# The last block of zeros in ten short transfers on SyncE's queue, and the epilogue written out twice

## The chip, the cores and the metric

One Trainium2 chip, one core. The metric is the device time of one execution, in microseconds (us); lower is better. A profiled execution gives a trace of all engines and of the core's 16 DMA engines; its span begins and ends a little inside the measured time.

## The reference

The kernel computes one decode step of a small block and all its gradients: layer norm of x, attention of one query per head over the last W = 4096 rows of a key/value cache of 32768 rows, a squared-ReLU MLP as a gate, and the vector-Jacobian product of the whole.

```python
q = (xn @ wq).reshape(B, Sq, Hq, Dh)                    # B 2, Sq 1, D 512, Hq 32, Hkv 8, Dh 128
k, v = k_cache[:, :, Sk - W:], v_cache[:, :, Sk - W:]   # W 4096 of Sk 32768
s = softmax(q k^T * Dh**-0.5) v @ wo
g = silu(relu(xn @ w1 + b1)**2 @ w2 + b2)               # w1 512 x 1792, w2 1792 x 512
out = x + s * g
grads = vjp(out, (x, k_cache, v_cache, wq, wo, w1, b1, w2, b2))(grad_out)
```

The outputs are out_0 (the forward result), out_1 (gradient of x), out_2 and out_3 (gradients of the two caches), out_4 (wq), out_5 (wo), out_6 and out_7 (w1, b1), out_8 and out_9 (w2, b2). All are bf16. out_2 and out_3 have the caches' size, 2 x 8 x 32768 x 128 each; only the last 4096 rows of each head take part in the attention, so the other 28672 rows (ZR in the code) of each of the 32 (output, batch, head) blocks are zeros that have to be written.

## The kernel before

The kernel is written in a tile language: instructions of one engine run in the order in which a scheduler put them, semaphores are placed by it, and writes to one output tensor, or reuse of one tile, are kept in order by waits.

**The zeros.** A tile of zeros, zt, lies in SBUF (L80). At the start 31 of the 32 zero blocks are queued from GpSimd (POOL), each as one or several DMAs, through the helper zf (L101), which keeps their handles in sw_fill. At most eight of them are in flight, by eight semaphores, so POOL's queue is fed for most of the run. The thirty-second block, the last head of out_3, is written by one SP DMA at the very end of the program (L641): 128 partitions by 4 repeats by 7168 elements. It is told to be issued after the store of out_6 (issue_after) and depends on the last but one fill of POOL (sw_fill[-2]).

**The work.** Weights are loaded on SP's queue, then four rounds go over the heads in groups of four. A round loads a slice of V and K (SP, L217), computes scores and gradients, and stores the slices of out_3 and out_2 (ACT's queue, L422). In the last round the output row, the MLP's backward pass and small outputs follow.

**The end.** After the rounds, ACT's queue stores out_4 from the tile wq (L581). Then come, in the program's text:

- L583 to L587: 32 matmuls of one 128x512 tile each; each result goes through one of three PSUM buffers (ps_o) into the tile wo by evac, which alternates between ACT (L157) and DVE (L159); ACT's queue stores wo as out_5 (L587).
- L589 to L602: a tile dw in the buffer of V's slices; in two halves, 7 transposes and a copy (L597, L598), and 7 transposes and a strided copy (L601, L602), through one PSUM buffer (ps_m).
- L605 to L610: 14 matmuls and evac into w2T; SP stores it as out_8 (L610).
- L611 to L616: 16 matmuls and evac into dw.
- L618 to L634: the layer norm's backward pass on small 128x8 tiles (dxnT, prodT, t1), with two sums over partitions by bsum (L165, L166) and four transposes (L177); SP stores the row as out_1 (L634).
- L636: SP stores dw as out_6; L641: SP writes the last zeros.

The scheduler mixes these: the layer norm part (L618 to L634) runs before most of the 32 matmuls of out_5. On SP the order is L634 (out_1), L610 (out_8), L636 (out_6), L641 (zeros).

Of the kernel before, what the change touches and what calls it, by code (L numbers as in the profile page):

```python
# [9 lines left out]
ALU = mybir.AluOpType  # L10
AX = mybir.AxisListType
BF16 = mybir.dt.bfloat16
F32 = mybir.dt.float32
# [3 lines left out]
def kernel(  # L17
# [24 lines left out]
    nc = tc.nc  # L42
    P = 128
    B, _, D = A_x.shape
    _, HKV, SK, DH = A_k_cache.shape
    N = A_wq.shape[1]
# [3 lines left out]
    F = B_w1.shape[1]  # L50
    FK = F // P
    DK = D // P
    NJ = N // P
# [3 lines left out]
    NCB = W // PB  # L57
# [11 lines left out]
    dma_store = nc.scalar  # L69
# [5 lines left out]
    ps_m = ctx.enter_context(tc.tile_pool(name="ps_m", bufs=1, space=PSUM))  # L75
    ps_o = ctx.enter_context(tc.tile_pool(name="ps_o", bufs=3, space=PSUM))

    ZR = SK - W
    ZG = 112
    zt = const.tile([P, ZG * DH], mybir.dt.uint8, name="zt")  # L80
    nc.vector.memset(zt[:].bitcast(F32), 0.0)

    ident_bf = const.tile([P, P], BF16, name="ident_bf")
    make_identity(nc, ident_bf[:])
    ident_f = const.tile([P, P], F32, name="ident_f")
    make_identity(nc, ident_f[:])

    sw_fill = []

    def zf(o, q, r0, nent, rows, rep=1):  # L90
        b, hk = divmod(q, HKV)
        nr = nent * rows * rep
        v = o[b, hk, r0:r0 + nr, :]
        w = rows * DH
        if w > ZG * DH:
            v = v.bitcast(F32)
            w //= 2
        v = v.rearrange("(r p g) d -> p r (g d)", p=nent, g=rows)
        st = 4 if nent < 16 else 1
        zs = zt[0:nent * st:st, 0:w].unsqueeze(1).to_broadcast([nent, rep, w])  # L100
        sw_fill.append(nc.gpsimd.dma_start(out=v, in_=zs))  # L101
        return r0 + nr

    ZQ = 2 * B * HKV
    zparts = [(out_2, q) for q in range(B * HKV)] + [(out_3, q) for q in range(B * HKV)]
# [12 lines left out]
    for qi in range(ZQ - 1):  # L118
        r = 0
        whole = (P, ZR // P, 1) if qi in zlong else (P, ZG, ZR // (P * ZG))  # L120
        for n, rows, rep in zshort.get(qi, (whole,)):
            r = zf(*zparts[qi], r, n, rows, rep)
# [8 lines left out]
    goT = const.tile([P, DK, B], F32, name="goT")  # L131
    xnT_f = const.tile([P, DK, B], F32, name="xnT_f")
    xnT = const.tile([P, DK, B], BF16, name="xnT")
    rstdb = const.tile([P, B], F32, name="rstdb")
    xn_bf = const.tile([B, D], BF16, name="xn_bf")
    w1T = const.tile([P, FK, D], BF16, name="w1T")
    w2T = const.tile([P, DK, F], BF16, name="w2T")
    rT = const.tile([P, FK, B], F32, name="rT")
    h2T_bf = const.tile([P, FK, B], BF16, name="h2T_bf")
# [3 lines left out]
    ds_rows = const.tile([B, D], BF16, name="ds_rows")  # L143
# [4 lines left out]
    dxqT = const.tile([P, DK, B], F32, name="dxqT")  # L148
# [3 lines left out]
    def evac(out_ap, in_ap, eng=None):  # L152
        if eng is None:
            eng = "act" if (evac_flip[0] % 2 == 0) else "dve"
            evac_flip[0] += 1
        if eng == "act":
            nc.scalar.copy(out=out_ap, in_=in_ap)  # L157
        else:
            nc.vector.tensor_copy(out=out_ap, in_=in_ap)  # L159

    def bsum(out_ap, in_t):
        pp = ps_m.tile([P, B], F32, tag="m")
        nk = in_t.shape[1]
        for k in range(nk):
            nc.tensor.matmul(pp[:, :], lhsT=ones_f[:, :], rhs=in_t[:, k, :], start=(k == 0), stop=(k == nk - 1))  # L165
        nc.vector.tensor_scalar_mul(out=out_ap, in0=pp[:, :], scalar1=1.0 / D)  # L166

    def kb(t2):
        return t2.unsqueeze(1).to_broadcast([P, DK, B])

    def pk_rows(t):
        return t.rearrange("b (p k) -> b k p", k=DK)

    def to_rows(src_T, dt, ident, pool=ps_m, tag="m"):
        tpp = pool.tile([B, DK, P], dt, tag=tag)
        for k in range(DK):
            nc.tensor.transpose(tpp[:, k, :], src_T[:, k, :], ident)  # L177
        return tpp

    wq = wts.tile([P, DK, N], BF16, name="wq")  # L180
    wo = wts.tile([P, NJ, D], BF16, name="wo")
# [23 lines left out]
    kvp = attn.enter_context(tc.tile_pool(name="kvp", bufs=1))  # L205
# [14 lines left out]
    with tc.tile_pool(name="pw", bufs=1) as pw:  # L220
# [14 lines left out]
        tp = ps_m.tile([P, DK, B], BF16, tag="m")  # L235
# [3 lines left out]
        tp = ps_m.tile([P, DK, B], BF16, tag="m")  # L239
# [21 lines left out]
        tp = to_rows(xnT, BF16, ident_bf[:, :])  # L261
# [3 lines left out]
        for fk in range(FK):  # L265
            for k in range(DK):
                nc.tensor.matmul(hps[:, fk, :], lhsT=w1[:, k, fk:F:FK], rhs=xnT[:, k, :],
                                 start=(k == 0), stop=(k == DK - 1))
        hBT = pw.tile([P, FK, B], F32, name="hBT")
        nc.vector.tensor_tensor(out=hBT[:], in0=hps[:], in1=b1T[:].unsqueeze(2).to_broadcast([P, FK, B]),  # L270
                                op=ALU.add)
# [3 lines left out]
        for dk in range(DK):  # L275
            for fk in range(FK):
                nc.tensor.matmul(ups[:, dk, :], lhsT=w2[:, fk, dk:D:DK], rhs=h2T_bf[:, fk, :],
                                 start=(fk == 0), stop=(fk == FK - 1))
        uT = pw.tile([P, DK, B], F32, name="uT")
        nc.vector.tensor_tensor(out=uT[:], in0=ups[:], in1=b2T[:].unsqueeze(2).to_broadcast([P, DK, B]),  # L280
                                op=ALU.add)
# [15 lines left out]
        tp = to_rows(dsT_bf, BF16, ident_bf[:, :])  # L297
# [4 lines left out]
        for j0 in range(0, NJ, JG):  # L302
            woT = pw.tile([P, JG, DK, P], BF16, tag="woT", bufs=2)
            for half in range(2):
                tp = ps_t.tile([P, 8, P], BF16, tag="pt")
                for jj in range(8):
                    j, dk = divmod(half * 8 + jj, DK)
# [3 lines left out]
            for dk in range(DK):  # L311
                nc.tensor.matmul(dops[0:B, :, :], lhsT=dsT_bf[:, dk, :], rhs=woT[:, :, dk, :],
                                 start=(dk == 0), stop=(dk == DK - 1))
            evac(do_rows[:].rearrange("b (p j) -> b j p", j=NJ)[:, j0:j0 + JG, :], dops[0:B, :, :])
        tp = ps_m.tile([P, HQ, B], BF16, tag="m")
# [5 lines left out]
        for n0 in range(0, N, 512):  # L321
            qps = ps_o.tile([P, 512], F32, tag="o")
            for k in range(DK):
                nc.tensor.matmul(qps[0:B, :], lhsT=xnT[:, k, :], rhs=wq[:, k, n0:n0 + 512],
                                 start=(k == 0), stop=(k == DK - 1))
            nc.scalar.mul(out=q_rows[:, n0:n0 + 512], in_=qps[0:B, :], mul=SCALE)
        tp = ps_m.tile([P, HQ, B], BF16, tag="m")
# [11 lines left out]
        for g0 in range(0, len(jobs), 8):  # L339
            grp = jobs[g0:g0 + 8]  # L340
            tp = ps_t.tile([P, 8, P], BF16, tag="pt")
            for j, (src, _, _, _) in enumerate(grp):
                nc.tensor.transpose(tp[:, j, :], src, ident_bf[:, :])
            j = 0
            while j < len(grp):
                dst, idx, off = grp[j][1], grp[j][2], grp[j][3]
                n = 1
# [9 lines left out]
    epi = attn.enter_context(tc.tile_pool(name="epi", bufs=1))  # L357
# [72 lines left out]
    for r in range(NR):  # L430
# [36 lines left out]
        if r == NR - 1:  # L467
            o_rows = tring[0:B, 0:N]
            for h0 in range(0, HQ, 8):
                tp = ps_t.tile([B, 8, P], BF16, tag="pt")  # L470
# [3 lines left out]
            tp = ps_s.tile([P, NJ, B], BF16, tag="sd")  # L474
# [9 lines left out]
            tp = ps_s.tile([P, DK, B], F32, tag="sd")  # L484
# [13 lines left out]
            tp = to_rows(outT, F32, ident_f[:, :], ps_s, "sd")  # L498
# [15 lines left out]
            tp = to_rows(duT_bf, BF16, ident_bf[:, :], ps_s, "sd")  # L514
            du_rows = zz[0:B, D:2 * D]
# [3 lines left out]
            for fk in range(FK):  # L519
                for dk in range(DK):  # L520
                    nc.tensor.matmul(hps[:, fk, :], lhsT=w2T[:, dk, fk * P:(fk + 1) * P], rhs=duT_bf[:, dk, :],
                                     start=(dk == 0), stop=(dk == DK - 1))
            dhBT = epi.tile([P, FK, B], F32, name="dhBT")
            nc.vector.scalar_tensor_tensor(out=dhBT[:], in0=hps[:], scalar=2.0, in1=rT[:], op0=ALU.mult, op1=ALU.mult)
            dhBT_bf = epi.tile([P, FK, B], BF16, name="dhBT_bf")
# [8 lines left out]
            for k in range(DK):  # L534
                for fk in range(FK):
                    nc.tensor.matmul(xps[:, k, :], lhsT=w1T[:, fk, k * P:(k + 1) * P], rhs=dhBT_bf[:, fk, :],
                                     start=(fk == 0), stop=(fk == FK - 1))
            dxnT = epi.tile([P, DK, B], F32, name="dxnT")
# [13 lines left out]
        b, h0 = rounds[r]  # L552
        for hk in range(h0, h0 + NP) if b == B - 1 else ():
            xps = ps_m.tile([P, DK, B], F32, tag="m")
            for half in range(2):
                wqT = wsl.tile([P, 2, DK, P], BF16, tag="wqT")
                tp = ps_t.tile([P, 8, P], BF16, tag="pt")
                for jj in range(8):
                    i, k = divmod(half * 8 + jj, DK)
                    n0 = (hk * REP + i) * DH  # L560
                    nc.tensor.transpose(tp[:, jj, :], wq[:, k, n0:n0 + DH], ident_bf[:, :])
                evac(wqT[:].rearrange("q i k p -> q (i k p)"), tp[:].rearrange("q a p -> q (a p)"))
                for k in range(DK):
                    for i in range(2):
                        nc.tensor.matmul(xps[:, k, :], lhsT=wqT[:, i, k, :], rhs=dqT_all[:, hk * REP + half * 2 + i, :],
                                         start=(half + k + i == 0), stop=(half == 1 and k == DK - 1 and i == 1))
# [4 lines left out]
            tp = ps_m.tile([B, REP, P], BF16, tag="m")  # L571
# [4 lines left out]
            for k in range(DK):  # L576
                wps = ps_o.tile([P, REP * DH], F32, tag="o")
# [5 lines left out]
    for j in range(NJ):  # L583
        wps = ps_o.tile([P, D], F32, tag="o")
# [4 lines left out]
    dw = kvp.tile([P, NCB * DH], BF16, tag="v")  # L589
    dw1_st = dw[:, 0:DK * F].rearrange("p (k f) -> p k f", k=DK)  # L590
    h2_rows = dw[0:B, DK * F:DK * F + F].rearrange("b (j p) -> b j p", j=FK)
    dhB_rows = dw[0:B, DK * F + F:DK * F + 2 * F]
    for half in range(2):
        f0, f1 = half * (FK // 2), (half + 1) * (FK // 2)
        tp = ps_m.tile([B, FK // 2, P], BF16, tag="m")
# [3 lines left out]
        tp = ps_m.tile([B, FK // 2, P], BF16, tag="m")  # L599
# [5 lines left out]
    dw2_st = w2T[:].rearrange("p k f -> p (k f)").rearrange("p (j d) -> p j d", j=FK)  # L605
    for fk in range(FK):
        wps = ps_o.tile([P, D], F32, tag="o")
# [3 lines left out]
    for k in range(DK):  # L611
        for n0 in range(0, F, 512):
            n = min(512, F - n0)
            wps = ps_o.tile([P, 512], F32, tag="o")
# [4 lines left out]
    m1b = epi.tile([P, B], F32, name="m1b")  # L619
    bsum(m1b[:], dxnT)  # L620
    prodT = epi.tile([P, DK, B], F32, name="prodT")
    nc.vector.tensor_tensor(out=prodT[:], in0=dxnT[:], in1=xnT_f[:], op=ALU.mult)
    m2b = epi.tile([P, B], F32, name="m2b")
    bsum(m2b[:], prodT)
    t1 = epi.tile([P, DK, B], F32, name="t1")
# [5 lines left out]
    tp = to_rows(t1, F32, ident_f[:, :])  # L631
    gx = dw[0:B, DK * F + 2 * F:DK * F + 2 * F + D]
# [2 lines left out]

    last = nc.sync.dma_start(out=out_6.rearrange("(p k) f -> p k f", k=DK), in_=dw1_st)  # L636
    b, hk = divmod(zparts[ZQ - 1][1], HKV)
    v = out_3[b, hk, 0:ZR, :].rearrange("(r p g) d -> p r (g d)", p=P, g=ZG // 2)
    zs = zt[:].bitcast(BF16).unsqueeze(1).to_broadcast([P, 2 * ZR // (P * ZG), ZG * DH // 2])
    with tc.issue_after(last.ins):  # L640
        fin = nc.sync.dma_start(out=v, in_=zs)  # L641
# [30 lines left out]
```

## Time and profile before

| | us |
|---|---|
| median of 2 runs (766.26 and 766.47) | 766.37 |
| the profiled execution, its own time | 766.29 |
| its span | 764.5 |
| PE busy in the span | 399.7 (52%) |
| DVE busy | 275.8 (36%) |
| ACT busy | 214.5 (28%) |
| POOL busy | 35.1 (5%) |

What the DMA queues moved, from part 3 of the page (packets, megabytes, time of their packets as a share of 16 engines' span); q0 is POOL's queue, q1 SP's, q10 ACT's:

```profile
q0 software_dynamic: 8000, 227.55, 70.4%
q1 hardware_dynamic: 2696, 56.63, 19.3%
q10 hardware_dynamic: 1736, 41.95, 13.5%
```

An engine's busy share is an average over stages. The table of 40 slices shows each engine, and the mean of the 16 DMA engines, in tenths of the slice. A timeline row has the start, the length, the engine, the line, the operation and its operands; an entry such as "ACTq L587 DMA_DIRECT2D" is the issue of a transfer by an engine's sequencer. A row of waits names who waited, for whom, how long in total, how often, and the longest. The sizes of the transfers at the end are 4096 KB (out_4 and out_5 each), 1792 KB (out_8 and out_6 each), 2 KB (out_1) and 7168 KB (the zeros).

### The profile page before, as it was taken

The page shows a single profiled execution, that of the slowest core. Times are in us where ns is not written, and L with a number is a line of the kernel's source. Part 1 is how long each engine was busy: PE and PEld are TensorE (multiplying, and loading weights), DVE is VectorE, ACT ScalarE, POOL GpSimd, SP SyncE. Part 2 cuts the span into 40 slices and gives each one's busy share as a digit, 9 for nine tenths or more (in the row PEclk, how much of TensorE's full clock was granted, in tenths as well). Part 3 has the DMA queues.
Part 4 walks back from the last instruction along what each step waited for, and adds up shares of the span by engine and source line. Part 5 has one row for each costly group of instructions (what it writes and reads, how often), then busy time and mean ns, then how long its engine had stood idle before and what let it go on. Part 6 is the DMA issues. An engine that isn't in the chain of part 4 may idle for free.

```text
span 764.5 us, 9399 instructions
## 1 busy us (share of the span) xinstructions
PE 399.7 (52%) x4118; PEld 261.8 (34%) x4118; DVE 275.8 (36%) x483; ACT 214.5 (28%) x313; POOL 35.1 (5%) x67
## 2 busy tenths in 40 slices
PE   0166774848503766870486683017645938759100
PEld 0153363734102654430275430016543424232000
DVE  3034252355501346450254653003343515567100
ACT  0034441145500124560122553002142307316100
POOL 3000010010000000000000000000000000000000
PEclk9998898968755995785599577559876957555555
DMA  9999999999999999999999999999999999999998
GB/s 360 433 425 427 442 422 430 438 426 425 429 428 438 427 446 430 413 427 435 435 427 440 427 433 438 420 433 429 437 430 436 430 440 430 418 438 425 436 417 379
DMA packets 12473, 326.73 MB, mean 427 GB/s; under 512 B 2898, under 2 KB 2906, under 8 KB 2934
## 3 DMA queue, kind: packets, MB, share of 16 engines
q0 software_dynamic: 8000, 227.55, 70.4%
q1 hardware_dynamic: 2696, 56.63, 19.3%
q10 hardware_dynamic: 1736, 41.95, 13.5%
q8 instruction: 32, 0.52, 0.3%
q14 instruction: 9, 0.07, 0.0%
HBM read 45.62 MB, written 280.50 MB: 427 GB/s over the span
## 4 chain that ended last, share of the span: by engine, by line
PE 33%; DMA 32%; DVE 14%; ACT 7%; issue 6%; ACTq 0%; DVEq 0%; SPq 0%
DMA out_dram<-nat 13%; DMA nat<-in_A_v_cache_dram 8%; DMA nat<-in_A_k_cache_dram 8%; PE ov L418 5%; PE s_ps L391 4%; PE tp L384 4%; DMA b_bf<-in_B_b_dram 4%; DVE tring L159 3%; PE dp_ps L391 2%; ACT p_bf L452 2%; ACT nat L157 2%; DVE ds_bf L465 2%; DVE nat L159 2%; PE wps L585 2%; PE ps L407 1%
## 5 line engine op out<-in xcount | busy, mean ns | idle before, releaser
L384 PE MATMUL tp<-pperm,nat 128*128 128x128 bf16 x1024 | 81.9, 228 | 136.4 <-DMA nat<-in_A_v_cache_dram 117.3
L159 DVE COPY tring<-tp 128x1024 bf16<-128x1024 bf16 (+1 forms) x98 | 65.5, 689 | 177.9 <-PE tp L384 168.3
L384 PEld LDWEIGHTS <-nat 128*128 128x128 bf16 x1024 | 70.8, 102 | 142.9 <-DMA nat<-in_A_v_cache_dram 119.3
L157 ACT CAST nat<-ov 128x512 bf16<-128x512 f32 x160 | 87.4, 590 | 61.9 <-PE ov L418 61.2
L157 ACT COPY tring<-tp 128x1024 bf16<-128x1024 bf16 (+1 forms) x34 | 34.4, 1011 | 239.7 <-PE tp L384 223.1
L159 DVE CAST nat<-ov 128x512 bf16<-128x512 f32 x96 | 65.7, 690 | 54.1 <-PE ov L418 51.4
L391 PEld LDWEIGHTS <-zz 128*128 128x128 bf16 x512 | 49.6, 100 | 37.3 <-issue 31.3
L101 POOL DMA_DIRECT2D out_dram<-zt x58 | 33.5, 581 | 529.3 <-DMA out_dram<-zt 526.1
L418 PE MATMUL ov<-bd,ds_bf 128*128 128x512 bf16 x128 | 49.2, 459 | 5.6 <-DVE nat L159 3.7
L418 PE MATMUL ov<-bd,p_bf 128*128 128x512 bf16 x128 | 48.6, 452 | 4.3 <-DVE nat L159 1.4
L391 PE MATMUL dp_ps<-tring,zz 128*128 128x256 bf16 x256 | 39.2, 284 | 12.1 <-DVE tring L159 6.9
L391 PE MATMUL s_ps<-tring,zz 128*128 128x256 bf16 x256 | 39.0, 275 | 10.9 <-DVE tring L159 9.9
L407 PE MATMUL ps<-t,nat 128*128 128x16 bf16 x1024 | 29.0, 174 | 13.7 <-DVE bd L372 6.8
L407 PEld LDWEIGHTS <-nat 128*128 128x128 bf16 x1024 | 28.9, 104 | 16.6 <-issue 11.4
L159 DVE CAST wq<-wps 128x512 bf16<-128x512 f32 x16 | 11.0, 690 | 42.4 <-PE wps L578 42.2
L399 PE MATMUL tp<-ident_bf,p_bf 128*128 128x128 bf16 x64 | 7.5, 312 | 34.9 <-ACT p_bf L452 34.9
L452 ACT ACTIVATE p_bf<-e_sb,rl 32x512 bf16<-32x512 f32 x16 | 22.8, 1424 | 3.4 <-DVE rl L449 3.3
L157 ACT CAST wq<-wps 128x512 bf16<-128x512 f32 x16 | 9.3, 586 | 50.6 <-PE wps L578 50.6
L465 DVE SCALAR_TENSOR_TENSOR ds_bf<-dp_ps,delta,p_bf 32x512 bf16<-32x512 f32 x16 | 21.8, 1360 | 0.2
L418 PEld LDWEIGHTS <-ds_bf 128*128 128x128 bf16 x128 | 12.9, 107 | 20.5 <-issue 18.2
L418 PEld LDWEIGHTS <-p_bf 128*128 128x128 bf16 x128 | 12.7, 108 | 19.5 <-issue 16.4
L399 PEld LDWEIGHTS <-p_bf 128*128 128x128 bf16 x64 | 6.5, 145 | 36.0 <-ACT p_bf L452 36.0
(195 smaller groups left out, 437.6 us busy)
## 6 DMA issues: line engine op xcount, KB each, us to landing
out_dram<-zt POOLq DMA_DIRECT2D x23, 7168.0 KB, 101.3
out_dram<-nat ACTq DMA_DIRECT2D x8, 4096.0 KB, 41.4
out_dram<-zt POOLq DMA_DIRECT2D x7, 3584.0 KB, 63.4
nat<-in_A_v_cache_dram SPq DMA_DIRECT2D x4, 4096.0 KB, 32.6
nat<-in_A_k_cache_dram SPq DMA_DIRECT2D x4, 4096.0 KB, 27.3
out_dram<-zt SPq DMA_DIRECT2D x1, 7168.0 KB, 52.2
out_dram<-zt POOLq DMA_DIRECT2D x2, 3488.0 KB, 64.6
out_dram<-zt POOLq DMA_DIRECT2D x1, 6120.0 KB, 85.8
```

What stands on the lines that cost most here:

```text
L101: sw_fill.append(nc.gpsimd.dma_start(out=v, in_=zs))
L157: nc.scalar.copy(out=out_ap, in_=in_ap)
L159: nc.vector.tensor_copy(out=out_ap, in_=in_ap)
L384: nc.tensor.transpose(tp[:, j, :], nat[:, g * CC + half * CH + j, :], pperm[:].rearrange("p b k -> p (b k)"))
L391: nc.tensor.matmul(out_ps[:, half * CH * PB:(half + 1) * CH * PB], lhsT=zbuf[:, pr, o:o + R], rhs=tT[:, :, pr, :], start=(g == 0 and pr == ...
L399: nc.tensor.transpose(tp[:, cc, :], src[:, half * CH + cc].rearrange("r k b -> r (k b)"), ident_bf[:, :])
L407: nc.tensor.matmul(ps[:], lhsT=nat[:, g * CC + half * CH + cc, :], rhs=cols[half][:, cc, :, g, :], start=(half == 0 and g == 0 and cc == 0 ...
L418: nc.tensor.matmul(ov[:], lhsT=src[:, cc].rearrange("r k b -> r (k b)"), rhs=bd[:, gh * 4:(gh + 1) * 4, :], start=True, stop=True)
L452: nc.scalar.activation(out=p_bf[rb, :, :, pr], in_=e_sb[rb], func=ACT.Copy, scale=rl[rb, 0:1])
L465: nc.vector.scalar_tensor_tensor(out=ds_bf[rb, :, :, pr], in0=dp_c[rb], scalar=delta[rb, 0:1], in1=p_bf[rb, :, :, pr], op0=ALU.subtract, o ...
L585: nc.tensor.matmul(wps[:], lhsT=o_rows[:, j:N:NJ], rhs=ds_rows[:, :], start=True, stop=True)
```

## The change

After the store of out_6 the new text writes the last head's zeros by ten DMAs on SP: one over 128 partitions with three repeats of 56 rows, one over 128 with 53 rows, and eight over 1, 7, 12, 13, 14, 15, 8 and 9 partitions (every eighth of the tile's) with 1, 2, 3, 4, 5, 6, 14 and 1 rows each. Together they are the same 28672 rows. Each is told to be issued after the one before it.

Behind them the new text has the end of the kernel once more, from the 32 matmuls of out_5 to the store of out_6, with lines of its own (L651 to L705), and then the old zero DMA, now at L710. So out_5, out_8, out_6, out_1 and the zeros are computed or written twice, to the same places. In the second pass dxqT is added to dxnT a second time (L687), so the second out_1 is made of a dxnT that holds dxqT twice. Nothing of the old text is removed.

```diff
     last = nc.sync.dma_start(out=out_6.rearrange("(p k) f -> p k f", k=DK), in_=dw1_st)
     b, hk = divmod(zparts[ZQ - 1][1], HKV)
+    zb = zt[:].bitcast(BF16)
+    r = 0
+    for n, g, rep, st in ((P, 56, 3, 1), (P, 53, 1, 1), (1, 1, 1, 8), (7, 2, 1, 8), (12, 3, 1, 8), (13, 4, 1, 8), (14, 5, 1, 8), (15, 6, 1, 8),
+                          (8, 14, 1, 8), (9, 1, 1, 8)):
+        v = out_3[b, hk, r:r + n * g * rep, :].rearrange("(r p g) d -> p r (g d)", p=n, g=g)
+        zs = zb[0:n * st:st, 0:g * DH].unsqueeze(1).to_broadcast([n, rep, g * DH])
+        with tc.issue_after(last.ins):
+            fin = nc.sync.dma_start(out=v, in_=zs)
+        if r == 0:
+            tc.add_manual_dep(fin.ins, sw_fill[-2].ins.name,
+                              mybir.DependencyInfo(mybir.DependencyClass.Sync, mybir.DependencyReason.DATA))
+        last = fin
+        r += n * g * rep
+    assert r == ZR, (r, ZR)
+    for j in range(NJ):
+        wps = ps_o.tile([P, D], F32, tag="o")
+        nc.tensor.matmul(wps[:], lhsT=o_rows[:, j:N:NJ], rhs=ds_rows[:, :], start=True, stop=True)
+        evac(wo[:, j, :], wps[:])
+    dma_store.dma_start(out=out_5.rearrange("(p j) m -> p j m", j=NJ), in_=wo[:])
+
+    dw = kvp.tile([P, NCB * DH], BF16, tag="v")
...
+    for half in range(2):
...
+            nc.tensor.transpose(tp[:, j, :], h2T_bf[:, f0 + j, :], ident_bf[:, :])
+        nc.vector.tensor_copy(out=h2_rows[:, f0:f1, :], in_=tp[:])
...
+            nc.tensor.transpose(tp[:, j, :], dhBT_bf[:, f0 + j, :], ident_bf[:, :])
+        nc.vector.tensor_copy(out=dhB_rows.rearrange("b (p j) -> b j p", j=FK)[:, f0:f1, :], in_=tp[:])
...
+    nc.sync.dma_start(out=out_8.rearrange("(p j) d -> p j d", j=FK), in_=dw2_st)
...
+    nc.vector.tensor_tensor(out=dxnT[:], in0=dxnT[:], in1=dxqT[:], op=ALU.add)
...
+    nc.sync.dma_start(out=out_1.rearrange("b s d -> (b s) d"), in_=gx)
+
+    last = nc.sync.dma_start(out=out_6.rearrange("(p k) f -> p k f", k=DK), in_=dw1_st)
+    b, hk = divmod(zparts[ZQ - 1][1], HKV)
     v = out_3[b, hk, 0:ZR, :].rearrange("(r p g) d -> p r (g d)", p=P, g=ZG // 2)
     zs = zt[:].bitcast(BF16).unsqueeze(1).to_broadcast([P, 2 * ZR // (P * ZG), ZG * DH // 2])
     with tc.issue_after(last.ins):
         fin = nc.sync.dma_start(out=v, in_=zs)
```

In the order of the built program SP issues, after the first out_1, out_8 and out_6: the second out_1 (L703), out_8 (L679) and out_6 (L705), the ten zero DMAs (L645), and L710. ACT issues the second out_5 (L656) between its copies of the second pass. The semaphores that the new instructions wait for: the first copies into wo on ACT and DVE, the landing of the first out_5; the first copy into the second dw (L667), the landing of the first out_1 and out_6; the last six of the ten zero DMAs, the landing of an earlier DMA that used the same semaphore (for the ninth the first of the ten, for the tenth the second); L710, the landing of all ten.

More of the change, by code (lines that the diff above doesn't have):

```diff
@@ new lines @@
+    assert r == ZR, (r, ZR)
[5 more added lines that the diff above has]
+    dw = kvp.tile([P, NCB * DH], BF16, tag="v")
+    dw1_st = dw[:, 0:DK * F].rearrange("p (k f) -> p k f", k=DK)
+    h2_rows = dw[0:B, DK * F:DK * F + F].rearrange("b (j p) -> b j p", j=FK)
@@ new lines @@
+    dhB_rows = dw[0:B, DK * F + F:DK * F + 2 * F]
+    for half in range(2):
+        f0, f1 = half * (FK // 2), (half + 1) * (FK // 2)
+        tp = ps_m.tile([B, FK // 2, P], BF16, tag="m")
+        for j in range(FK // 2):
+            nc.tensor.transpose(tp[:, j, :], h2T_bf[:, f0 + j, :], ident_bf[:, :])
+        nc.vector.tensor_copy(out=h2_rows[:, f0:f1, :], in_=tp[:])
+        tp = ps_m.tile([B, FK // 2, P], BF16, tag="m")
+        for j in range(FK // 2):
+            nc.tensor.transpose(tp[:, j, :], dhBT_bf[:, f0 + j, :], ident_bf[:, :])
+        nc.vector.tensor_copy(out=dhB_rows.rearrange("b (p j) -> b j p", j=FK)[:, f0:f1, :], in_=tp[:])
@@ new lines @@
+    dw2_st = w2T[:].rearrange("p k f -> p (k f)").rearrange("p (j d) -> p j d", j=FK)
+    for fk in range(FK):
+        wps = ps_o.tile([P, D], F32, tag="o")
+        nc.tensor.matmul(wps[:], lhsT=h2_rows[:, fk, :], rhs=du_rows, start=True, stop=True)
+        evac(dw2_st[:, fk, :], wps[:])
+    nc.sync.dma_start(out=out_8.rearrange("(p j) d -> p j d", j=FK), in_=dw2_st)
+    for k in range(DK):
+        for n0 in range(0, F, 512):
+            n = min(512, F - n0)
+            wps = ps_o.tile([P, 512], F32, tag="o")
+            nc.tensor.matmul(wps[:, 0:n], lhsT=xn_bf[:, k:D:DK], rhs=dhB_rows[:, n0:n0 + n], start=True, stop=True)
+            evac(dw1_st[:, k, n0:n0 + n], wps[:, 0:n])
@@ new lines @@
+    nc.vector.tensor_tensor(out=dxnT[:], in0=dxnT[:], in1=dxqT[:], op=ALU.add)
+    m1b = epi.tile([P, B], F32, name="m1b")
+    bsum(m1b[:], dxnT)
+    prodT = epi.tile([P, DK, B], F32, name="prodT")
+    nc.vector.tensor_tensor(out=prodT[:], in0=dxnT[:], in1=xnT_f[:], op=ALU.mult)
+    m2b = epi.tile([P, B], F32, name="m2b")
+    bsum(m2b[:], prodT)
+    t1 = epi.tile([P, DK, B], F32, name="t1")
+    nc.vector.tensor_tensor(out=t1[:], in0=xnT_f[:], in1=kb(m2b[:]), op=ALU.mult)
+    nc.vector.tensor_tensor(out=t1[:], in0=dxnT[:], in1=t1[:], op=ALU.subtract)
@@ new lines @@
+    nc.vector.tensor_tensor(out=t1[:], in0=t1[:], in1=kb(m1b[:]), op=ALU.subtract)
+    nc.vector.tensor_tensor(out=t1[:], in0=t1[:], in1=kb(rstdb[:]), op=ALU.mult)
+    nc.vector.tensor_tensor(out=t1[:], in0=t1[:], in1=goT[:], op=ALU.add)
+    tp = to_rows(t1, F32, ident_f[:, :])
+    gx = dw[0:B, DK * F + 2 * F:DK * F + 2 * F + D]
+    nc.vector.tensor_copy(out=pk_rows(gx), in_=tp[:])
+    nc.sync.dma_start(out=out_1.rearrange("b s d -> (b s) d"), in_=gx)
+    last = nc.sync.dma_start(out=out_6.rearrange("(p k) f -> p k f", k=DK), in_=dw1_st)
```

## The prediction

> **What bounds the kernel now.** I read the page's table of 40 slices first, for which resource is never idle.
>
> ```profile
> DMA  9999999999999999999999999999999999999998
> GB/s 360 433 425 427 442 422 430 438 426 425 429 428 438 427 446 430 413 427 435 435 427 440 427 433 438 420 433 429 437 430 436 430 440 430 418 438 425 436 417 379
> HBM read 45.62 MB, written 280.50 MB: 427 GB/s over the span
> ```
>
> The DMA engines are 90% busy or more in every slice but the last, and the busiest compute engine (PE) only 52%. The kernel is bound by bytes; compute matters only if it delays the issue of a transfer when nothing else is queued. So next come the windows of the last 54 us, with compute beside DMA, and a window of the DMA queues there.
>
> ```profile
> core 0: us, PE busy (x) PEld busy (x) DVE busy (x) ACT busy (x) POOL busy (x), PEclk, DMA share, GB/s
> ...
> 711.00:720.00 9.00, 0.00 (x0) 0.00 (x0) 0.00 (x0) 0.00 (x0) 0.00 (x0) 0.50 1.02 436
> 720.00:730.00 10.00, 0.00 (x0) 0.00 (x0) 0.00 (x0) 0.00 (x0) 0.00 (x0) 0.50 1.03 437
> ...
> 745.00:750.00 5.00, 0.00 (x0) 0.00 (x0) 0.00 (x0) 0.00 (x0) 0.00 (x0) 0.50 1.02 436
> ```
>
> Compute is over at 711; 21.87 MB are still to move (DMA view, 711 to 764.5). From 744 to 750 only SP's queue (q1) moves bytes, 2.62 MB, so POOL's and ACT's queues are empty by then. The timeline says when the last transfers were issued, the waits of SP when they landed.
>
> ```profile
> 667.12 3.97 DVE L602 COPY dw<-tp 2x896 bf16<-2x896 bf16 x1 [0.40 <-PE tp L601]
> ...
> 696.63 0.35 ACTq L587 DMA_DIRECT2D out_dram<-wo  x1
> ...
> 704.18 0.33 SPq L610 DMA_DIRECT2D out_dram<-w2T  x1
> ...
> 710.84 0.33 SPq L636 DMA_DIRECT2D out_dram<-dw  x1
> 711.36 0.39 SPq L641 DMA_DIRECT2D out_dram<-zt  x1
> ```
>
> ```profile
> SPq L667 <- DMA out_dram<-zz: 27.1, 1, 27.1
> ...
> SPq L667 <- DMA out_dram<-zt: 17.0, 1, 17.0
> ...
> SPq L667 <- DMA out_dram<-wq: 4.3, 1, 4.3
> SPq L667 <- DMA out_dram<-dw: 3.0, 1, 3.0
> ```
>
> These are SP's closing waits, which begin at 711.8. Put end to end as 27.1, 4.3, 3.0, 17.0 they end at 738.9, 743.2, 746.2 and 763.2. The second agrees with out_5's own record (issued 696.63, landing after 46.6 us: 743.2). So out_5 lands at 743.2, out_6 at about 746.2, and the last fill, 7168 KB issued at 711.36, is what keeps DMA busy afterwards: 7.34 MB in 17.0 us, 432 GB/s. It lands at 763.6 (52.2 us after issue), 0.9 us before the span ends.
>
> **What the Trainium skill says.** "DMA: Bandwidth & Descriptors", section "Issuing engines are not separate DMA queues": DMAs started by SP, ACT and POOL run on the same 16 engines and interleave. The trace agrees: 437 GB/s with three queues (720 to 730), 436 with one (745 to 750). Same page, "Anatomy of one DMA — SWDGE (gpsimd) path": about 2.0 us fixed per DMA, most of it the wait for the last byte's receipt. The trace splits it for a hardware queue: the first load is issued at 0.74 and bytes flow from about 2.0 (1.3 us), and the last fill's final data packet is at about 762.7 against its landing at 763.6 (0.9 us); together 2.2 us, which I use. Same page, "Why a DMA increments its semaphore by 16 and not by 1": a hardware-queue DMA uses the largest number of engines up to 16 that divides its slowest dimension, so 7 rows use 7 engines; no row of this trace shows that.
>
> **The change, part by part.** The words speak of the last fill alone. The diff has more: after ten new fills (L645) it repeats the whole end of the kernel (out_5, out_8, out_6, out_1) and keeps the old fill, now L710. The order of the built program has both copies. Removed: nothing; the old fill moves to the end of SP's queue.
>
> (a) *Bytes.* Added are 4096 KB (out_5), 1792 (out_8), 1792 (out_6), 2 (out_1) and 7168 (ten fills): 14850 KB = 15.2 MB. At 432 GB/s: **+35.2 us**, with nothing to hide under, since DMA is full already.
>
> (b) *First pass.* In the built order seven transposes (L666) and two small DVE operations (L687, L691) slip in at about 683: 0.91 us by the like row L601, 0.17 each by L618. SP then issues the first out_6 at about 712 instead of 710.84. Free: three queues hold bytes past 740.
>
> (c) *A new wait, and the fill that covered it is gone.* The second pass refills wo, so its first copies on ACT and DVE wait for the first out_5 to have landed, 743.2. Behind them stand everything else on ACT and DVE and, through three PSUM buffers, PE. On SP the ten fills stand behind the second out_6 (L705), thus behind the whole second pass. After the first out_6's last bytes (746.2 less 0.9: 745.3) no queue holds anything.
>
> (d) *Second pass, from rows of the first, at the same 0.50 clock.* 32 wo copies: ACT's starts go from 686.49 to 695.42 in ten steps, 0.89 us a pair. The twelfth DVE copy ends about 743.2+11.1 = 754.3, then L667 0.6. The last four wo copies, held by transposes between the matmuls, end at 758.7. ACT issues the second out_5 after its next copy: 759.4. L671 (as L602, 3.97) to 762.7; copy, transposes, L667, transposes (0.91 twice, 0.6, overlap taken) to 765.2; L671 again to 769.2. The mean and variance chain as in the first pass, 677.7 to 685.3: 7.6 us, so 776.9. Remaining four pairs of out_8 copies at 0.89: 780.5, issue of the second out_8. Then 6.66 us (704.18 to 710.84): **second out_6 issued at 787.3**.
>
> DMA in that time: idle 745.3 to 760.7 (759.4+1.3), 15.4 us; out_5 4.19 MB, 9.7 us, to 770.4; idle to 781.8, 11.4 us; out_8 1.835 MB, 4.3 us, to 786.1; idle to 788.6, 2.5 us. **Idle 29.3 us.**
>
> (e) *The fills.* From 788.6 out_6 (1.835 MB), the 128x3x7168 fill (5.51 MB) and the 128x6784 one (1.74 MB) flow without a gap: 9.08 MB, 21.0 us, to 809.6. The short ones are 98 KB in all. Issues cost some 0.4 us each and lie under the flow. But the ninth waits for the semaphore of the first fill and the tenth for that of the second, which lands at 810.5. The tenth then takes 2.2: 812.7. SP issues L710 only when all ten have landed, since it writes the same rows: first byte 814.0, 17.0 us of bytes to 831.0, landed 831.9, span end 832.8. **Idle here 4.4 us.**
>
> Sum against the profiled execution: span 764.5 + 35.2 + 29.3 + 4.4 = 833.4, by the chain 832.8; I take 833. Around the span lie 766.29 - 764.5 = 1.8 us: **835 us**; the median of the two runs (766.37) is 0.1 above the profiled one. What no row shows: the fixed time of a DMA on a few engines, 1 to 4 us (it enters twice, since both the tenth and L710 start on idle queues): -2 to +4; the length of the second pass: as quick as DVE's copies alone, 0.69 for 0.89 on some 27 pairs, -5.4; as slow as the first from its first matmul (663.81 to 710.84, 47.0 instead of 44.1): +2.9. Engines that drain unevenly may move each start by a little, 2 us either way (a choice). All ends together: 825 to 844.
>
> **Rivals.**
> 1. *The second pass is covered and only the bytes count.* 766.3 + 35.2 = 802, and up to 8 us less if DMA's small losses (327 MB at 432 GB/s would take 756) were made up. It needs bytes queued between 746 and 788; the built order has the fills behind L705, against it. Chance 0.05; with a half-covered gap, 815 to 825, another 0.05.
> 2. *Waits pile up further*: engines that drain unevenly lengthen each of the landings in the chain (out_5, fill one, fill two, tenth, L710), or a pass that meets out_6's landing in L667 (746.2, before 754.3, so not expected to bind): 844 to 855. Chance 0.07.
> 3. *The other side: the change does no more than its words say*, one set of stores and short fills in place of the long one. Then only SP's tail grows: at least two dependent landings at 2.2 us, 766.3 + 4.4 = 771, within 2%. It decides if no second out_5, out_8, out_6 and no L710 is issued. Against it are the diff and the built order. Chance 0.02. No cover could bring the full change there: 15.2 MB would have to fit into 15.3 us.
>
> **How the numbers follow.** Forecast, 825 to 844: 0.81. Rival 1 with its half-way case 0.10, rival 2 0.07, rival 3 0.02. The predicted time is the likeliest case's, 835. The range 825 to 844 leaves out 0.19. Two per cent, about what a measurement can tell from no change, is 15.3 us: slower by more than that are all cases but rival 3: 0.98; same 0.015, faster 0.005.
>
> **What would show it.** Right: MB moved near 342; three near-empty stretches of DMA, about 745 to 761, 770 to 782 and 786 to 788; ACT and DVE waiting for out_dram<-wo until about 743; L656 issued near 759, L705 near 787, L710 near 813, and 17 us of SP's queue alone at the end. Wrong: DMA at 430 GB/s throughout (rival 1), no L710 (rival 3), L710 issued without waiting for the ten (2.2 us less and both flows joined), or a second pass much longer or shorter than 44 us.

## The result and the profile after

The changed kernel takes 834.09 us (two runs, 833.59 and 834.58) against 766.37 before: a ratio of 1.0884, 95% interval 1.0837 to 1.093. The forecast was 835, with a range of 825 to 844. The profiled execution has a span of 832.5 us. In three of the kernels below, one execution ran two to three per cent longer than the others (824.3, 793.88 and 792.73 us); these three are left out of the figures given.

First the page of the changed kernel, the DMA rows of its 40 slices and its bytes:

```profile
DMA  9999999999999999999999999999999999974398
GB/s 363 429 433 421 442 424 442 413 442 421 433 430 432 443 422 421 435 428 431 446 425 429 422 438 427 429 444 433 434 428 429 428 438 417 436 338 202 136 394 353
...
HBM read 45.62 MB, written 295.71 MB: 410 GB/s over the span
```

295.71 MB are written where it was 280.50: 15.2 MB more, the stores and zeros written twice. But the rate over the span has fallen from 427 to 410 GB/s, and nearly all of the fall lies in four of the 40 slices, the 36th to the 39th (a slice is 20.8 us long). Up to there the rows are much like those of before. So the time has two parts: more bytes, and a DMA that stands idle. The windows of the changed kernel show the holes (columns: stretch, its length, busy time of PE, PE loads, DVE, ACT and POOL, clock, DMA share, GB/s):

```profile
747.00:750.00 3.00, 3.00 (x8) 0.93 (x7) 2.42 (x4) 1.93 (x4) 0.00 (x0) 0.50 0.00 0
750.00:755.00 5.00, 5.00 (x13) 1.60 (x12) 3.94 (x7) 3.33 (x6) 0.00 (x0) 0.50 0.00 0
755.00:760.00 5.00, 5.00 (x16) 1.50 (x16) 3.46 (x6) 2.51 (x5) 0.00 (x0) 0.50 0.00 0
...
765.00:770.00 5.00, 1.44 (x8) 0.71 (x7) 4.60 (x4) 0.57 (x1) 0.00 (x0) 0.50 0.98 419
...
772.00:777.00 5.00, 3.75 (x15) 2.37 (x15) 1.55 (x8) 0.59 (x1) 0.00 (x0) 0.50 0.00 0
...
800.00:808.00 8.00, 0.00 (x0) 0.00 (x0) 0.00 (x0) 0.00 (x0) 0.00 (x0) 0.50 1.01 430
```

Read the last column beside the PE, DVE and ACT columns. From 747 to 760 compute works and not one byte moves; from 765 to 770 the second out_5 flows; from 772 to 777 nothing moves again; from 800 to 808 DMA is full and compute is over. In the kernel before such windows had bytes and no compute, because the last zeros were queued there. Why compute is so late is on ACT's timeline of the changed kernel:

```profile
743.97 1.07 ACT L157 CAST wo<-wps 128x512 bf16<-128x512 f32 x2 [29.90 <-DMA out_dram<-wo]
...
759.64 0.34 ACTq L656 DMA_DIRECT2D out_dram<-wo  x1
```

The second pass's first copy into wo waited 29.90 us for the first out_5 to land. And SP's timeline of the changed kernel shows what stands behind that pass:

```profile
777.90 0.26 SPq L703 DMA_DIRECT2D out_dram<-dw  x1
781.10 0.34 SPq L679 DMA_DIRECT2D out_dram<-w2T  x1
787.77 0.33 SPq L705 DMA_DIRECT2D out_dram<-dw  x1
788.15 23.32 SPq L645 DMA_DIRECT2D out_dram<-zt  x10
812.81 0.40 SPq L710 DMA_DIRECT2D out_dram<-zt  x1
```

SP's waits of the changed kernel (who, for whom: total us, times, longest) name the landings at the end:

```profile
SPq L736 <- DMA out_dram<-zt: 17.9, 1, 17.9
SPq L645 <- DMA out_dram<-zt: 12.6, 2, 8.9
...
SPq L710 <- DMA out_dram<-zt: 1.1, 1, 1.1
```

Two of the ten zero DMAs waited for another one, then L710 for the tenth, then the program for L710.

### The profile page after: what moved, and what is told of

It reads as the page before. It is cut to its first block, busy times and chain, and to the rows that moved or that the text cites. A ratio compares the mean times of both kernels' runs of the same rounds, so it can differ in the third digit from the quotient of the medians.

```text
span 832.5 us, 9725 instructions
## 1 busy us (share of the span) xinstructions
PE 443.4 (53%) x4219; PEld 280.0 (34%) x4228; DVE 307.0 (37%) x528; ACT 232.7 (28%) x344; POOL 35.0 (4%) x67
## 3 DMA queue, kind: packets, MB, share of 16 engines
HBM read 45.62 MB, written 295.71 MB: 410 GB/s over the span
## 4 chain that ended last, share of the span: by engine, by line
DMA 34%; PE 33%; DVE 14%; ACT 7%; issue 5%; ACTq 0%; DVEq 0%; SPq 0%
DMA out_dram<-nat 11%; DMA nat<-in_A_k_cache_dram 8%; DMA nat<-in_A_v_cache_dram 7%; DMA out_dram<-wo 5%; PE ov L418 5%; PE s_ps L391 4%; PE tp L384 4%; DMA b_bf<-in_B_b_dram 4%; DVE tring L159 3%; PE dp_ps L391 2%; ACT p_bf L452 2%; ACT nat L157 2%; DVE ds_bf L465 2%; PE wps L585 2%; PE wps L654 2%
## 5 line engine op out<-in xcount | busy, mean ns | idle before, releaser
L391 PE MATMUL dp_ps<-tring,zz 128*128 128x256 bf16 x256 | 40.9, 293 | 11.6 <-DVE tring L159 6.4
L159 DVE CAST wo<-wps 128x512 bf16<-128x512 f32 x32 | 22.3, 696 | 38.7 <-DMA out_dram<-wo 29.9
L157 ACT CAST wo<-wps 128x512 bf16<-128x512 f32 x32 | 18.7, 586 | 61.0 <-DMA out_dram<-wo 29.9
L654 PE MATMUL wps<-ds_rows,tring 2*128 2x512 bf16 x32 | 14.9, 606 | 29.5 <-ACT wo L157 29.4
```

The source lines that it names most:

```text
L391: nc.tensor.matmul(out_ps[:, half * CH * PB:(half + 1) * CH * PB], lhsT=zbuf[:, pr, o:o + R], rhs=tT[:, :, pr, :], start=(g == 0 and pr == ...
L654: nc.tensor.matmul(wps[:], lhsT=o_rows[:, j:N:NJ], rhs=ds_rows[:, :], start=True, stop=True)
```

## The experiments

Two theories were set against each other. Theory 1 is the prediction's: 35 us are bytes, and the rest is DMA standing idle, because the second pass waits for the first out_5 and the zeros are queued behind the pass, plus waits for landings at the end. Theory 2: the time is bytes plus what short DMAs over few engines cost by themselves. The kernel before ran beside the experiments at 766.4 to 766.5 us.

### The cover given back: the zeros ahead of the second pass

```diff
+    with tc.issue_after(fin.ins):
+        nc.sync.dma_start(out=out_8.rearrange("(p j) d -> p j d", j=FK), in_=dw2_st)
...
+    with tc.issue_after(fin.ins):
+        nc.sync.dma_start(out=out_1.rearrange("b s d -> (b s) d"), in_=gx)
...
+    with tc.issue_after(fin.ins):
+        last = nc.sync.dma_start(out=out_6.rearrange("(p k) f -> p k f", k=DK), in_=dw1_st)
```

> The second pass's stores of out_1, out_8 and out_6 are told to be issued on SP after the ten zero DMAs, so the zeros go out at about 714 and no byte or instruction is added or taken away. Theory 1 (DMA stood idle because the zeros were queued behind the second pass): the zeros fill the idle stretch from 745 to 763, the second out_5 follows to 772, out_8 runs 782 to 787, out_6 starts at 789 and the last zero DMA joins it: 789.1 + 21.2 = 810.3, landed 811.2, span 812.1, time 813.8 us. Theory 2 (the time is the bytes plus a cost of the short DMAs on few engines, wherever they stand): unchanged, 834.

Measured: 812.89 us (four runs, 812.34 to 813.16; ratio 1.0604, 1.0588 to 1.062). The same bytes and instructions take 21.2 us less in another order on SP's queue; on PE, DVE and ACT the order in the trace is that of the changed kernel. The windows of this kernel:

```profile
745.00:760.00 15.00, 14.97 (x38) 4.51 (x36) 11.43 (x17) 9.20 (x16) 0.00 (x0) 0.50 1.02 434
...
772.00:780.00 8.00, 6.24 (x21) 2.96 (x22) 4.40 (x11) 2.19 (x4) 0.00 (x0) 0.50 0.05 16
```

The stretch that had 0 GB/s has 434 beside busy engines; the later hole, before the second out_8, is still there, as forecast. Theory 2 falls here as the main cause.

### The wait taken away: the second pass in tiles of its own

```diff
-        evac(wo[:, j, :], wps[:])
+        evac(wo2[:, j, :], wps[:])
-    dma_store.dma_start(out=out_5.rearrange("(p j) m -> p j m", j=NJ), in_=wo[:])
+    dma_store.dma_start(out=out_5.rearrange("(p j) m -> p j m", j=NJ), in_=wo2)
...
-    dw = kvp.tile([P, NCB * DH], BF16, tag="v")
+    dw = kvp.tile([P, NCB * DH], BF16, tag="k")
...
-    dw2_st = w2T[:].rearrange("p k f -> p (k f)").rearrange("p (j d) -> p j d", j=FK)
+    dw2_st = w1T[:].rearrange("p j d -> p (j d)").rearrange("p (j d) -> p j d", j=FK)
```

Here wo2 is a view of the tile wq, whose store is done early.

> The second pass puts its results in other tiles (out_5 in the tile of wq, out_8 in that of w1T, its dw in the buffer of K), which are free by about 711 or earlier, so it does not wait for the landing of the first out_5 at 743. Theory 1: the pass starts at about 714 and issues its out_6 near 758 to 764, while DMA is still full; only bytes and the landings at the end remain, 766.4 + 35.2 + 4.4 = 806, 804 to 810. Theory 2 (bytes and short DMAs): unchanged, 834. Theory 3 (the second pass itself is slow, 44 us, at the low clock, wherever it starts): it would show as a pass of over 44 us, but also near 806.

Measured: a ratio of 1.0556 (1.0517 to 1.0595), which is 809 us, with runs from 806.55 to 811.7. Within the forecast's 804 to 810, at its upper end. Its windows tell why:

```profile
745.00:750.00 5.00, 4.88 (x11) 1.29 (x10) 4.02 (x6) 3.15 (x7) 0.00 (x0) 0.50 0.35 151
750.00:755.00 5.00, 4.07 (x9) 1.07 (x9) 2.83 (x5) 2.48 (x5) 0.00 (x0) 0.50 0.98 419
```

One hole of about 3 us is left. Without the wait the scheduler put pieces of the second pass into the first: the second out_1 is issued at 723.71, ahead of the first out_8, and the first out_6 only at 733.58. So the second out_5 is issued at 748.39, when the queues have run dry. Also here no byte was taken away, and 25 us are gone. But two things changed at once, the wait and the order of the passes, so the 25 us are not the price of the wait alone.

### Less to write: one of the two sets of zeros left out

Without L710 (its lines deleted; every output is still written once or more):

> The last zero DMA (L710), which writes the same rows a second time, is left out. Theory 1: the span ends when the tenth short DMA has landed, at about 812.7, plus 0.9: 813.6, time 815.3 us, 18.8 less (17.0 of bytes and one fixed time of about 2). Theory 2: 7.34 MB at 432 GB/s less: 817.1.

Measured: 815.4 us (815.11 to 815.81), the forecast being 815.3. Without the ten zero DMAs and with L710:

> The ten zero DMAs are left out, the second pass and the old zero DMA stay, so the zeros are written once. Theory 1: L710's place is right behind the second out_6 at 788.2, out_6 and zeros flow from 789.1 for 21.2 us, landed 811.2, span 812.1, time 813.8 us: 20.3 less, of which 17.0 are bytes and 3.3 the two landings that the ninth and tenth short DMA and L710 waited for. Theory 2: the bytes, 17.0, and on top whatever DMAs on few engines cost; if that is a large part of the 67.7 us, well under 810.

Measured: 813.35 us (812.42 to 813.63), forecast 813.8. So leaving out L710 saves 18.7 us and leaving out the ten saves 20.7: 17.0 are the bytes of a set of zeros, the rest landings that something waits for. Neither is near the 67.7 of the whole, so the short DMAs are not the main cost.

### Fewer bytes inside the hole

First the second out_5 was computed and not stored (the line of L656 deleted).

> The second out_5 is still computed into wo but not stored: 4.19 MB, 9.7 us of DMA at 432 GB/s, are left out. Theory 1 (between 744 and 788 the chain of compute that waited for the first out_5 sets the time, and DMA only fills holes in it): the time stays, 834 within 1.5. Theory 2 (every byte counts): 824.4.

Measured: 829.49 us (829.31 to 829.78), 4.6 less: neither 834 nor 824.4. SP's timeline of this kernel:

```profile
782.97 0.33 SPq L704 DMA_DIRECT2D out_dram<-dw  x1
...
785.94 20.72 SPq L645 DMA_DIRECT2D out_dram<-zt  x10
```

The second out_6 is issued at 782.97 instead of 787.77, 4.8 us earlier. Without that store the scheduler put the layer norm's sums among the copies of out_6 (DVE's first sum, at 775.83, comes after the last copy of out_8) and not ahead of the last copies of out_8, so the pass was another one. If half the row is stored, the order on PE, DVE and ACT stays that of the changed kernel:

```diff
-    dma_store.dma_start(out=out_5.rearrange("(p j) m -> p j m", j=NJ), in_=wo[:])
+    dma_store.dma_start(out=out_5.rearrange("(p j) m -> p j m", j=NJ)[:, 16:NJ, :], in_=wo[:, 16:NJ, :])
```

> Of the second out_5 only the second half of each partition's row is stored: 2.10 MB, 4.9 us of DMA at 432 GB/s, are left out, and PE, DVE and ACT keep the order of instructions of the changed kernel (without the store altogether they did not). Theory 1 (the chain of compute sets the time there): 834.1 within 0.8. Theory 2 (every byte counts): 829.2.

Measured: 833.96 us (832.65 to 835.1). 2.10 MB less, worth 4.9 us of a full DMA, change nothing: the bytes of the second out_5 flow inside a hole that the chain of compute holds open. Part of that chain are DVE's strided copies, for which PE's transposes and sums wait (waits of the changed kernel):

```profile
PE pp L165 <- DVE dw L671: 3.5, 1, 3.5
...
PE tp L666 <- DVE dw L671: 2.9, 1, 2.9
```

### Only what the words say

The ten zero DMAs instead of the old one, and no second pass:

> What the words of the change say and no more: the ten zero DMAs in place of the old one, no second pass, no L710. Theory 1: the zeros flow as before, but the tenth DMA waits for the landing of the second, so the end is one fixed time later: 766.4 + 2.2 = 768.6, 768 to 769.5. Theory 2: if the few-engine DMAs even out engines that end late, below 766; if they cost by themselves, over 771.

Measured: a ratio of 1.0026 (1.0015 to 1.0037), median 768.55 us, 2.0 more than the 766.53 before, as expected. This is the prediction's rival 3 as a kernel. Then with the eight short ones ahead of the two long ones, alone and in the changed kernel:

```diff
-    for n, g, rep, st in ((P, 56, 3, 1), (P, 53, 1, 1), (1, 1, 1, 8), ..., (9, 1, 1, 8)):
+    for n, g, rep, st in ((1, 1, 1, 8), ..., (9, 1, 1, 8), (P, 56, 3, 1), (P, 53, 1, 1)):
```

> As the words of the change say, without the second pass and L710, and with the eight short zero DMAs ahead of the two long ones. No short DMA waits for a long landing, the bytes are those of before. Theory 1: the time of before, 766.4 within 0.7. Theory 2 (few-engine DMAs cost by themselves): over 768.

> The eight short zero DMAs stand ahead of the two long ones; bytes, number of DMAs and partitions are the same. The two long ones then share semaphores with short ones that have landed early, and only L710 waits for a long landing. Theory 1 (each landing waited for on an empty queue costs about 2.2 us): one landing less, 834.1 - 2.2 = 831.9. Theory 2 (few-engine DMAs cost by themselves, wherever they stand): 834.

Both expectations missed: 769.56 us (769.0 to 770.23) where 766.4 was expected, and 835.72 (835.03 to 836.12) where 831.9 was. The windows of the first of these kernels, and two of SP's waits in it:

```profile
744.00:746.00 2.00, 0.00 (x0) 0.00 (x0) 0.00 (x0) 0.00 (x0) 0.00 (x0) 0.50 0.64 260
746.00:748.00 2.00, 0.00 (x0) 0.00 (x0) 0.00 (x0) 0.00 (x0) 0.00 (x0) 0.50 0.03 11
748.00:750.00 2.00, 0.00 (x0) 0.00 (x0) 0.00 (x0) 0.00 (x0) 0.00 (x0) 0.50 0.83 344
```

```profile
SPq L645 <- DMA out_dram<-wo: 18.7, 1, 18.7
...
SPq L645 <- DMA out_dram<-dw: 2.1, 1, 2.1
```

The expectation had left out that the short ones share semaphores with the stores before them. The sixth waits 18.7 us for out_5, the eighth 2.1 us for out_6. It is issued at 746.59, when the queues are empty, and the first long one stands behind it on SP and goes out at 747.38: a hole of about 3 us at 745.

In the changed kernel there is a hole too, from 793 to 796, but for another reason:

```profile
788.01 8.21 SPq L645 DMA_DIRECT2D out_dram<-zt  x10
...
794.00:796.00 2.00, 0.00 (x0) 0.00 (x0) 0.00 (x0) 0.00 (x0) 0.00 (x0) 0.50 0.10 27
```

Here no zero DMA waits: SP's waits have no row for L645. SP issues the ten without a pause, but issuing one takes it 0.28 to 1.39 us, and the eight short ones take 7.2 us together. The first long one goes out at 795.23, and by then the bytes of out_6 are through. So neither kernel tests a removed landing; one hole was exchanged for another.

Last, six short ones in place of eight, behind the long ones, so that with eight semaphores no zero DMA waits for another:

```diff
-        ..., (1, 1, 1, 8), (7, 2, 1, 8), (12, 3, 1, 8), (13, 4, 1, 8), (14, 5, 1, 8), (15, 6, 1, 8), (8, 14, 1, 8), (9, 1, 1, 8)
+        ..., (12, 2, 1, 8), (12, 3, 1, 8), (13, 4, 1, 8), (14, 5, 1, 8), (15, 6, 1, 8), (8, 14, 1, 8)
```

> The changed kernel with six short zero DMAs in place of eight (12, 12, 13, 14, 15 and 8 partitions, the same 384 rows), so that no zero DMA shares a semaphore with another one; L710 still waits for all. Theory 1: one landing on an empty queue less than in the changed kernel, 834.1 - 2.2 = 831.9, 831.4 to 832.6. Theory 2 (short DMAs cost by their number or few engines, no wait in it): at most a quarter of such a cost is gone, 833.5 or more.

> Only the zero DMAs are changed, no second pass and no L710, and with six short ones behind the two long ones, so that none of them waits for a zero DMA. Theory 1: nothing is left of the change that could cost, the time of before, 766.5 within 0.5. Theory 2 (short DMAs even out engines that end late): 765.5 or less. Theory 3 (they cost by themselves): 768 or more.

Measured: 833.48 us (832.79 to 833.97) where 831.9 was expected, and a ratio of 1.0014 (1.0008 to 1.0021), median 767.56, where 1.0 was. Both missed. In the kernel without a second pass about 1 us of the 2.0 is gone and about 1.2 stays; in the changed kernel 0.6 are gone by the medians, where 2.2 were expected. The DMA view of the changed kernel with six short ones, in the quarter and half microseconds 808.5 to 809, 809.25 to 809.5 and 809.5 to 810, and then three of its issues (KB, us from issue to landing, where the view has it), say what stays:

```profile
DMA packets 16, 0.22 MB, mean 434 GB/s; under 512 B 0, under 2 KB 0, under 8 KB 0
DMA packets 88, 0.04 MB, mean 163 GB/s; under 512 B 46, under 2 KB 88, under 8 KB 88
DMA packets 71, 0.06 MB, mean 114 GB/s; under 512 B 41, under 2 KB 63, under 8 KB 71
...
out_dram<-zt SPq DMA_DIRECT2D x1, 1696.0 KB, 22.1
out_dram<-zt SPq DMA_DIRECT2D x1, 22.5 KB, 16.4
...
811.18 0.39 SPq L710 DMA_DIRECT2D out_dram<-zt  x1
```

The last long packets start before 809 at 434 GB/s; the short rows come behind them, at 163 and 114 GB/s, and their 98 KB take from 809.2 to 810.0. The second long DMA, issued at 787.90, lands at 810.0 too. But the short one of 22.5 KB, issued at 794.50, lands at 810.9, and L710, which waits for all, is issued at 811.18. The landing records of this trace have the six short ones one after another, about 0.17 us apart, from 810.18 to 811.06. So 1.2 us pass between the landing of the last long zeros and L710, after the short rows' bytes have moved too: it is their landings in a row. That the 1.2 us of the kernel without a second pass are the same is not shown.

With the ten and no second pass, the tenth is the last to land, as expected (at 765.86 by the landing records of that trace), but the other short ones are down only at 765.19; so leaving the tenth out gives back only a part of the 2.0 us. About 1.2 us are what is left of theory 2. None of the versions beats the kernel before.

## Why the prediction was right

**What bounds the kernel** held: wherever long transfers were queued, DMA moved some 430 GB/s, and where none were, compute set the time. The sum holds term by term. From 745 to 788.6 the changed kernel moved 6.26 MB, 14.5 us at 432 GB/s, so 29.1 of these 43.6 us were idle (forecast 29.3). From 788.6 to the first byte of L710, at 813.7, it moved 9.18 MB, 21.2 us, so 3.9 were idle (forecast 4.4). With 35.2 for the bytes that is 68.2 us; the span grew by 68.0.

**(a) Bytes.** 15.2 MB more are written. The price of 432 GB/s fits the two sets of zeros (17.0 us each, plus landings).

**(b) First pass.** Free, as put. In the profiled execution the first out_6 is issued at 714.19, later than the 712 of the working, and out_5 still lands near 743. In the first experiment's trace the whole first pass is 19 us later (out_5 issued at 718.86, out_6 at 733.10), and the wait for out_5 still ends at 743.29: the time of landing hardly depended on the time of issue.

**(c) The wait and the lost cover.** Forecast at 743.2, the first copy starts at 743.97. The first experiment shows the lost cover (21.2 us by order alone). The second shows that without the wait most of the idle time goes (25 us), though in another order of the two passes.

**(d) The second pass.** Forecast issues: out_5 759.4, out_8 780.5, out_6 787.3; measured 759.64, 781.10 and 787.77. Each duration came from a row of the first pass at the same clock, including DVE's two strided copies of nearly 4 us, which hold PE and with it everything else. The idle time was right for the reason given: halving the transfer inside it changed nothing. Two small errors cancel here. The start was put 0.8 us early. And the first byte was put 1.3 us after an issue, but it comes after 0.8 to 0.9 us (out_5 issued at 759.64, first bytes at 760.5; out_6 at 787.77 and 788.6; L710 at 812.81 and 813.7). The row that the 1.3 was read from shows less, too: the first load was issued at 0.74, and SP's queue moves bytes from about 1.77, not 2.0.

**(e) The fills.** L710 was forecast at about 813 and issued at 812.81; the span ends at 832.5, forecast 832.8. The chain was the one forecast: the second zero DMA lands, the tenth is issued at 810.72 and L710 at 812.81, 2.1 us later where 2.2 were put. What the working put at nothing is a second chain beside it. It had the short rows at their bytes, 98 KB under the flow, but by the landing records of the changed kernel they land one after another behind the long zeros, the ninth at 811.75, the tenth at 812.55. In this kernel that is hidden behind the tenth. It is why 0.6 us were gained with no tenth, by the medians, and not 2.2. The issues were put at 0.4 us each; those of the first six short ones take 1.06 to 1.39, which lies under the flow here as forecast.

**Rivals.** Rival 1 (802, everything covered) is a property of the order: 812.9 and 809 were reached by giving back the cover or taking away the wait. Rival 3, only the words, was put at 771 and is 768.6: the working counted two dependent landings of 2.2 us beyond the old end, and the zeros' own landing is already in the time of before, so one was counted too many. Rival 2 was not met.

The Trainium skill's fixed time of about 2 us for a DMA ("DMA: Bandwidth & Descriptors", "Anatomy of one DMA — SWDGE (gpsimd) path") agrees with the 2.1 us of the tenth, though the page gives it for transfers issued from GpSimd, and this one is issued from SP and moves 2.2 KB.

## What to carry to other kernels

In a kernel whose DMA is full to the end, the transfer queued last is also the cover for whatever compute is still to come: before adding work at the end, look what will be queued while it runs, and on which queue that stands behind it. Price added work by the hole it opens as well as by its bytes, from the landing that its first instruction waits for. When a program has more DMAs at its end than semaphores to give them, the later ones wait for the landing of earlier ones, and whatever stands behind such a waiting DMA on the same engine waits with it. Short DMAs ahead of a long one also hold it back by the time that it takes to issue them.

## What was not expected of the hardware

Short DMAs of 98 KB in all, queued behind long ones on the same queue, cost about 1.2 us at the end (767.56 against 766.40) even when no zero DMA waits for another. Where it was looked at, they landed one after another, about 0.17 us apart, after their bytes had moved. Issuing a short one took SP up to 1.39 us, against 0.46 for the long one behind the eight (both in the changed kernel with the short ones ahead). And splitting the zeros into long and short transfers did not shorten the end of the kernel in any of the three forms tried (767.56, 768.55, 769.56).
